# A unit's second scan and its B placed ahead of the sums' eviction, and the last pair's output reordered, in a fused Mamba-2 and SiLU kernel

## The chip, the cores and the metric

The kernel runs on one core of a Trainium2 chip. The metric is the device time of one execution in microseconds. The kernel before takes 362.78 us, the median of three runs (362.65, 362.78 and 364.97). The execution that the profile shows took 364.51 us as a whole; its span in the profile is 362.7 us.

## The reference

Two blocks follow each other. The first is a chunked state-space scan with decays `a` over 768 positions for 4 batches and 8 heads (head size 32, state size 16). The second is a feed-forward block with a SiLU over the 3072 tokens, with 256 features and 2048 hidden ones.

```
cum = cumsum(log a);  L[i, j] = exp(cum[i] - cum[j]) for i >= j
M = (C B^T) * L
y = M x + (C state) * exp(cum)                     # within a chunk, and from the state
state = exp(cum[-1]) * state + sum_j exp(cum[-1] - cum[j]) B[j] x[j]
...
h = y @ w_in;  g = h * sigmoid(h);  out = g @ w_out    # per token, y with all heads side by side
```

The activations and the output are 32-bit floats; the weights come as 64-bit floats and are read as pairs of 32-bit words, from which ACT, DVE and GpSimd make 32-bit floats.

## The kernel before, in words

The tokens are cut into 12 **units** of 256 positions, three to a batch; two units are a **pair** of 512 tokens. The scan of a unit makes the feed-forward block's input `XF`. The first pair (P = 0) has a path of its own. For pairs 1 to 5 a loop `step(s)` runs over s = 0 to 82: s = 16 (P - 1) + f handles the 128 hidden features number f of pair P, and in the gaps it is interleaved with the scan of the two units of the next pair, called "a" and "b". The order of the instructions on each engine is the order in which this Python code emits them; nothing reorders it. The table `PLAN` names by f what is emitted for the scan, `FIRST` does so for "2B" alone.

**The products.** Each matrix product with exact 32-bit operands is split in three single-pass ones. A value v is split into a high part h, a low part l = v - h, and a third operand d, a sum of the two with other weights. With h h', l l' and d d' the wanted product comes out as a weighted sum. In `step`:

- `s1_h` (L526) and `s1_d` (L518) are the first matrix product, on TensorE; `hp` is its PSUM tile, which ACT rescales between the two (L520).
- `s1_g` (L534, L536) is SiLU and the high part of its result on ACT; `s1_gl` (L540) and `s1_gd` (L544) make the low part and the d part. In some steps (`ASIDE`: f = 2, 4, 5, 6, 10, 15) `s1_gl` is on GpSimd, else on DVE.
- `s2` (L558, L559) adds h h' and l l' of the second product into the two PSUM tiles `OA[P][m]`, three steps later (`LAG`). `s2_d` (L572) adds d d' of it into the tile `B2[P]`, which covers four PSUM banks. While scans need these banks, the d d' products of some steps are put off and collect in `PENDING`.

`B2` and the scan's tiles `gy` share these four banks, one tile at a time.

**The end of a pair.** When the sixteenth `s2` of a pair is due, `ends` is true: that is at f = 2 of the next pair, s = 18, 34, 50, 66 and, for the last pair, 82. `f_out` then evicts the sums on DVE. For pairs 1 to 4 the part of `B2` up to then was set aside at f = 8 by ACT as `SUM2` (`f_sum2`, L580), so that the bank could be used by the scan; L595 computes UP * OA - SUM2, and L602 subtracts what `B2` gathered since. For the last pair no `SUM2` exists, so ACT copies OA with its scale (L598) in place of L595, and L602 follows. `f_store` transposes the two results on DVE (L611) and stores each with four DMAs on the SP queue (L613). It comes at f = 5 for the pairs before the last, and at once for the last. For the first pair `f_out0` at s = 2 does it, with a copy on ACT (L584), transposes and stores.

**The scan of a unit.** `f_E1` is half of the E scan (a running product per head, L324, on DVE, 128 x 512 from the tile `ab`). For unit "a" the first half is emitted at f = 1 and the second at f = 3 ("2B" in `FIRST`); for "b" the first at f = 8 and the second at f = 9. Behind the second half comes `f_B` (L347), which makes BT from B and the last columns of E. BT is the weight of the state products `f_D0` (L390), which `PLAN` has at f = 3 (a) and f = 9 (b), behind `f_G` (L402). Then follow the state steps on DVE (L422), the product with E on DVE (`f_M`, L408), and the output products of `f_Y` (L442, L451) at f = 5 and 11. The loads of the next unit are emitted with their waits on the SP queue ("bL" at f = 1): `bn` waits until BT has been read, `ab` until the scan has been done.

Within `step`, the order before is: `s1_h`, `s1_d`; at an end the outstanding d d' products, `s2` and `f_out`; `s1_g`; else `s2` and, where due, `s2_d`; `f_sum2`; the `FIRST` part; `s1_gl`, `s1_gd`; the stores; the `PLAN` parts; splitting of weights.

Of the kernel before, what the change touches and what calls it, by code (L numbers as in the profile page):

```python
# [12 lines left out]
AF = mybir.ActivationFunctionType  # L13
ALU = mybir.AluOpType
# [14 lines left out]
UP = 4097.0  # L29
# [4 lines left out]
def kernel(  # L34
# [22 lines left out]
    nc = tc.nc  # L57
# [27 lines left out]
    def block(name, dtype=FP32):  # L85

        return blk.tile([128, 512], dtype, name=name, tag="blk", bufs=NB)

    def half(name):
        return ps_h.tile([128, 512], FP32, name=name, tag="h")  # L90

    def bank4(name="gy"):
        return ps_s.tile([128, 4, 512], FP32, name=name, tag="gy")

    def acc(name):
        return ps_a.tile([128, 512], FP32, name=name, tag="a")

    ab, bn, tbc, xt = ({} for _ in range(4))
# [40 lines left out]
    def load_unit(u):  # L139
        load_pa(u, nc.sync)  # L140
        if 0 < u < UPB:
            load_n(u, 1, nc.sync)
        else:
            load_t(u, 0, nc.sync)
            load_t(u, 1, nc.sync)
        load_n(u, 0, nc.sync)
        load_ab(u, nc.sync)
        load_x(u, nc.sync)
# [10 lines left out]
    def two(t):  # L159
        return t.rearrange("p (k f) -> p k f", k=2)  # L160
# [195 lines left out]
    def f_TP(u):  # L356
        tp = half("tp")
        for i, t in enumerate((bn[u],) if u == 0 else (bn[u], tbc.pop(u))):
            for k in range(2):
                nc.tensor.transpose(out=tp[:, 256 * i + 128 * k:256 * i + 128 * k + 128],  # L360
                                    in_=t[:, k].rearrange("p h n -> p (h n)"), identity=ident)
        BH[u] = sc.tile([128, UT], FP32, name="bh")
        nc.scalar.activation(BH[u], tp[:, 0:256], AF.Copy)
        if u > 0:
            CT[u] = tp[:, 256:512]

    def f_T2(u, e):
        if e == 0:
            CE[u] = sc.tile([128, 2, UT], FP32, name="ce")
        nc.scalar.activation(CE[u][:, e], CT[u], AF.Copy, scale=par[:, e:e + 1])  # L370
# [114 lines left out]
    GT, OA = {}, {}  # L485
# [28 lines left out]
    def s1_d(s):  # L514
        P, f = 1 + s // NF, s % NF
        HP[s] = half("hp")
        for kc in range(KC):
            nc.tensor.matmul(out=HP[s], lhsT=two(WD[f // 2])[:, kc, 128 * (f % 2):128 * (f % 2) + 128], rhs=XD[P][:, kc],  # L518
                             start=(kc == 0), stop=False, skip_group_check=True)
        nc.scalar.activation(HP[s], HP[s], AF.Copy, scale=-HALF / UP)  # L520
# [26 lines left out]
    B2, SUM2 = {}, {}  # L547

    def s2(s):

        P, f = 1 + s // NF, s % NF
        if f == 0:
            OA[P] = [acc("oa") for m in range(2)]
        n, r = 8 + f // 2, f % 2
        gh, gl = GH.pop(s), GL.pop(s)
        for m in range(2):
            ms = slice(128 * m, 128 * m + 128)
            nc.tensor.matmul(out=OA[P][m], lhsT=two(WH[n])[:, r, ms], rhs=gh, start=(f == 0), stop=False)  # L558
            nc.tensor.matmul(out=OA[P][m], lhsT=two(WL[n])[:, r, ms], rhs=gl, start=False, stop=(f == NF - 1))  # L559

    def s2_d(tiles):

        P = 1 + tiles[0] // NF
        fresh = P not in B2
        if fresh:
            B2[P] = bank4("b2")
        for s in tiles:
            f = s % NF
            n, r = 8 + f // 2, f % 2
            gd = GD.pop(s)  # L570
            for m in range(2):
                nc.tensor.matmul(out=B2[P][:, m], lhsT=two(WD[n])[:, r, 128 * m:128 * m + 128], rhs=gd,  # L572
                                 start=(fresh and s == tiles[0]), stop=True, skip_group_check=True)

    def f_sum2(P):

        b2 = B2.pop(P)
        SUM2[P] = [block("sum2") for m in range(2)]
        for m in range(2):
            nc.scalar.activation(SUM2[P][m], b2[:, m], AF.Copy, scale=HALF)  # L580
# [8 lines left out]
    def f_out(P):  # L589

        b2 = B2.pop(P)
        for m in range(2):
            o = block("o")
            if P in SUM2:
                nc.vector.scalar_tensor_tensor(out=o, in0=OA[P][m], scalar=UP, in1=SUM2[P][m],  # L595
                                               op0=ALU.mult, op1=ALU.subtract)
            else:
                nc.scalar.activation(o, OA[P][m], AF.Copy, scale=UP)  # L598
            OUT.append((P, m, o))
        for m in range(2):  # L600
            o = OUT[m][2]
            nc.vector.scalar_tensor_tensor(out=o, in0=b2[:, m], scalar=-HALF, in1=o, op0=ALU.mult, op1=ALU.add)  # L602

    def f_store():
        for P, m, o in OUT:
            store(P, m, o)
        OUT.clear()

    def store(P, m, o):
        r = block("ot")  # L610
        nc.vector.transpose(out=r, in_=o)  # L611
        for q in range(4):
            nc.sync.dma_start(  # L613
                out=bass.AP(tensor=out.tensor, offset=out.offset + 2 * UT * P * d_model + 128 * m + 32 * q,
                            ap=[[d_model, 32], [32 * d_model, 2 * UT // 32], [1, 32]]),
                in_=r[32 * q:32 * q + 32].rearrange("p (b d) -> p b d", d=32))
# [60 lines left out]
    def stage(u, what):  # L677
        for c in what:
            if c == "L":
                load_unit(u)  # L680
            elif c == "T":
                if 0 < u < UPB:
                    f_TP(u)
                else:
                    f_T(u, 0)
                    f_T(u, 1)
                f_T2(u, 0)
                f_T2(u, 1)
            elif c == "P":
                f_P(u)  # L690
            elif c in "12":
                f_E1(u, int(c) - 1, 2)
            elif c == "B":
                f_B(u)
            elif c == "C":
                f_C(u)
            elif c == "D":
                f_G(u)
                f_D0(u)
            elif c == "M":  # L700
                f_M(u, 0)
                f_M(u, 1)
            elif c == "S":
                f_S(u)
            elif c == "s":
                f_SM(u)
            elif c == "Y":
                f_Y(u)
                f_X(u)
            elif c == "h":  # L710
                f_xh(u)
            elif c == "l":
                f_xl(u)
            elif c == "d":
                f_xd(u)
# [17 lines left out]
    for text in ("m0 3:C12B 2:h h1 l0 d0 2:l b13 s14", "m1 3:D 2:d 4:L h2 l1 d1 b14 s15", "m2 3:SsM h3 l2 d2 b15",  # L733
# [4 lines left out]
    NP = NU // 2  # L738
# [1 line left out]

    PLAN = {0: ("aPC",), 1: ("a1", "bL"), 3: ("aD",), 4: ("aSsM",), 5: ("aY",), 6: ("ah", "bT"), 7: ("bPC",), 8: ("b1", "aL"),
            9: ("bD",), 10: ("bSsM",), 11: ("bY",), 12: ("bh", "ald"), 13: ("bld",), 15: ("aT",)}
    FIRST = {3: "a2B", 9: "b2B"}

    ASIDE = (2, 4, 5, 6, 10, 15)
    PENDING = []
# [3 lines left out]
    def step(s):  # L750

        last = NF * (NP - 1)
        t = s - LAG
        P, f = 1 + s // NF, s % NF
        ends = t >= 0 and t % NF == NF - 1
        scans = P + 1 < NP
        if t >= 0:
            PENDING.append(t)
        if s == 0:
            s1_d(0)  # L760

        if s < last:
            s1_h(s)
            if s + 1 < last:
                s1_d(s + 1)
        if ends:
            s2_d(PENDING)
            s2(t)
            PENDING.clear()
            f_out(1 + t // NF)  # L770
        if s < last:
            s1_g(s)
        if s < 2:
            f_s2(6 + s)
        if s == 2:
            f_out0(0)
            f_out0(1)
        if t >= 0 and not ends:
            s2(t)
        if PENDING and not (scans and (f < 6 or 9 <= f < 12)):  # L780
            s2_d(PENDING)
            PENDING.clear()
        if scans and f == 8:
            f_sum2(P)
        if scans and f in FIRST:
            stage(2 * P + 2 + "ab".index(FIRST[f][0]), FIRST[f][1:])
        if 1 <= s <= last:
            s1_gl(s - 1, nc.gpsimd if f in ASIDE and scans else nc.vector)
            s1_gd(s - 1)
        if ends and s >= last:  # L790
            f_store()
        if s >= last:
            return
        if t > 4 and t % NF == 2:
            f_store()
        if scans:
            for what in PLAN.get(f, ()):
                u = 2 * P + 2 + "ab".index(what[0])
                if f == 15 or what == "aL":
                    u += 2  # L800
                if u < NU:
                    stage(u, what[1:])
        if s in PARTS:
            w_h(PARTS[s])
        if s - 1 in PARTS:
            w_l(PARTS[s - 1])
            w_d(PARTS[s - 1])
# [34 lines left out]
```

## Time and profile before

| engine | busy us | share of 362.7 us |
|---|---|---|
| PE (matmul) | 333.4 | 92% |
| PEld (weight load) | 260.3 | 72% |
| DVE | 259.7 | 72% |
| ACT | 211.7 | 58% |
| POOL (GpSimd) | 64.4 | 18% |

A group's row in the profile gives line, engine, operation, what is written and read, count, busy time, mean ns, idle time of the engine ahead of these instructions and what ended it. These are the groups that the change touches:

```profile
L324 DVE TENSOR_TENSOR_SCAN E<-ab,diag 128x512 f32<-128x512 f32 x24 | 29.2, 1232 | 1.1 <-DMA ab<-a_zero 0.6 <-PE ab L331 0.5
L347 DVE TENSOR_TENSOR BT<-bn,E 128x256 f32<-128x256 f32 x12 | 8.8, 732 | 0.4
L595 DVE SCALAR_TENSOR_TENSOR o<-oa,sum 128x512 f32<-128x512 f32 x8 | 5.2, 686 | 10.3 <-PE oa L559 10.3
L580 ACT ACTIVATE sum<-b 128x512 f32<-128x512 f32 x8 | 4.3, 585 | 0.0
```

A busy PE isn't a PE at its peak, since matmuls are pipelined: a 128 x 512 product is recorded with some 0.39 us, while the next one starts 0.23 us later. The end of the span holds no matmuls: the last one starts at 353.29 us.

### The profile page before, as it was taken

How to read it: one execution, taken by the hardware profiler on the slowest of the kernel's cores; microseconds unless marked ns; L12 is line 12 of the kernel's file. 1: busy time of each engine (PE TensorE's matmuls, PEld its weight loads, DVE VectorE, ACT ScalarE, POOL GpSimd, SP SyncE). 2: the span in 40 equal slices, each digit the busy share in tenths (PEclk: the TensorE clock that was granted, in tenths of full speed). 3: DMA queues.
4: the chain of work that ended last, by engine and by line, in shares of the span. 5: the costliest groups of instructions: out<-in, count | busy, mean ns of one | idle time of the engine just before them, and what ended most of it. 6: DMA issues, size and time to landing. Idle time of an engine off the chain costs nothing.

```text
span 362.7 us, 7826 instructions
## 1 busy us (share of the span) xinstructions
PE 333.4 (92%) x3145; PEld 260.3 (72%) x3146; DVE 259.7 (72%) x430; ACT 211.7 (58%) x403; POOL 64.4 (18%) x56
## 2 busy tenths in 40 slices
PE   8888999897979999979999979999979999999990
PEld 3567787776747778757778757777758778788870
DVE  6969976995388998697865685865684863574442
ACT  3566576144348876747666637667636766656630
POOL 3225441220113011122101132101131101000000
PEclk9999999898989999999999989999989999999997
DMA  6875976521026240135330143420153000030003
GB/s 140 181 260 147 223 263 135 125 65 27 16 46 118 55 94 0 37 64 108 76 73 0 43 100 67 96 49 2 43 109 54 2 2 0 0 52 7 0 3 59
DMA packets 99339, 26.67 MB, mean 74 GB/s; under 512 B 87558, under 2 KB 92422, under 8 KB 99302
## 3 DMA queue, kind: packets, MB, share of 16 engines
q1 hardware_dynamic: 97222, 26.03, 31.7%
q8 instruction: 25, 0.41, 0.5%
q10 hardware_dynamic: 2080, 0.13, 0.4%
q14 instruction: 12, 0.10, 0.1%
HBM read 22.80 MB, written 3.34 MB: 72 GB/s over the span
## 4 chain that ended last, share of the span: by engine, by line
PE 67%; DVE 14%; SPq 6%; DMA 6%; issue 3%; ACT 1%; DVEq 0%; ACTq 0%
PE hp L526 21%; PE b L572 10%; PE hp L518 10%; PE oa L559 10%; PE oa L558 10%; DMA raw<-in_moe_w_out_dram 3%; DVE E L324 2%; PE oa L504 2%; SPq L121 2%; DVE wv L187 2%; PE gy L451 2%; DVE BT L347 2%; PE gy L442 1%; DVE wl L203 1%; DMA raw<-in_moe_w_in_dram 1%
## 5 line engine op out<-in xcount | busy, mean ns | idle before, releaser
L520 ACT ACTIVATE hp<-hp 128x512 f32<-128x512 f32 x80 | 46.6, 582 | 90.2 <-PE hp L518 89.9
L540 DVE TENSOR_TENSOR gl<-g,gh 128x512 fp32r<-128x512 f32 x56 | 38.6, 690 | 52.3 <-ACT gh L536 47.2
L540 POOL TENSOR_TENSOR gl<-g,gh 128x512 fp32r<-128x512 f32 x24 | 38.1, 1589 | 188.4 <-ACT gh L536 183.6
L526 PE MATMUL hp<-xh,wh 128*128 128x512 f32 x160 | 66.6, 416 | 2.6 <-ACT hp L520 2.6
L544 DVE SCALAR_TENSOR_TENSOR gd<-gh,g 128x512 fp32r<-128x512 f32 x80 | 57.8, 726 | 9.8 <-ACT gh L536 9.7
L526 PE MATMUL hp<-xl,wl 128*128 128x512 f32 x160 | 64.5, 403 | 0.0
L559 PE MATMUL oa<-gl,wl 128*128 128x512 f32 x160 | 64.4, 402 | 0.0
L558 PE MATMUL oa<-gh,wh 128*128 128x512 f32 x160 | 63.8, 399 | 0.0
L536 ACT ACTIVATE gh<-g 128x512 fp32r<-128x512 f32 x80 | 50.5, 632 | 2.9
L518 PE MATMUL hp<-xd,wd 128*128 128x512 f32 x160 | 52.1, 407 | 0.0
L534 ACT ACTIVATE g<-hp 128x512 f32<-128x512 f32 x80 | 47.5, 594 | 0.6 <-PE hp L526 0.6
L572 PE MATMUL b<-gd,wd 128*128 128x512 f32 x160 | 44.6, 391 | 0.0
L526 PEld LDWEIGHTS hp<-xh,wh 128*128 128x128 f32 x160 | 30.7, 192 | 12.8 <-ACT hp L520 5.4
L518 PEld LDWEIGHTS hp<-xd,wd 128*128 128x128 f32 x160 | 31.0, 194 | 7.7
L558 PEld LDWEIGHTS oa<-gh,wh 128*128 128x128 f32 x160 | 30.9, 193 | 7.8 <-ACT o L584 0.7
L559 PEld LDWEIGHTS oa<-gl,wl 128*128 128x128 f32 x160 | 30.8, 193 | 7.5
L572 PEld LDWEIGHTS b<-gd,wd 128*128 128x128 f32 x160 | 30.0, 188 | 6.8 <-DVE o L602 0.2
L526 PEld LDWEIGHTS hp<-xl,wl 128*128 128x128 f32 x160 | 30.7, 192 | 5.8
L491 PE MATMUL hp<-xf,w 128*128 128x256 f32 x128 | 30.2, 386 | 3.6 <-POOL w L192 2.1
L192 POOL TENSOR_TENSOR w<-wu,wv 128x512 uint32<-128x512 uint32 (+1 forms) x20 | 23.4, 1179 | 50.5 <-DVE wv L187 47.8
L504 PE MATMUL oa<-gT,w 128*128 128x256 f32 x128 | 31.0, 402 | 0.0
L491 PEld LDWEIGHTS hp<-xf,w 128*128 128x128 f32 x128 | 23.4, 190 | 9.2 <-POOL w L192 3.4
(80 smaller groups left out, 370.3 us busy)
## 6 DMA issues: line engine op xcount, KB each, us to landing
ab<-a_zero SPq DMA_DIRECT2D x40, 128.0 KB
raw<-in_moe_w_in_dram SPq DMA_DIRECT2D x8, 512.0 KB
raw<-in_moe_w_out_dram SPq DMA_DIRECT2D x8, 512.0 KB
xt<-in_x_dram SPq DMA_DIRECT2D x24, 128.0 KB
out_dram<-ot SPq DMA_DIRECT2D x48, 64.0 KB
bn<-in_B_dram SPq DMA_DIRECT2D x22, 64.0 KB
tbc<-in_C_dram SPq DMA_DIRECT2D x40, 32.0 KB
pz<-a_in SPq DMA_DIRECT2D x40, 32.0 KB
```

Of the source, the lines that this page charges most:

```text
L491: nc.tensor.matmul(out=hp[:, i], lhsT=two(w32[j])[:, kc, 128 * i:128 * i + 128], rhs=two(XF[u])[:, kc], start=(kc == 0), stop=(kc == KC - 1))
L504: nc.tensor.matmul(out=OA[0][m][:, UT * u:UT * u + UT], lhsT=two(w32[8 + j])[:, i, 128 * m:128 * m + 128], rhs=two(GT[u, j])[:, i], start= ...
L518: nc.tensor.matmul(out=HP[s], lhsT=two(WD[f // 2])[:, kc, 128 * (f % 2):128 * (f % 2) + 128], rhs=XD[P][:, kc], start=(kc == 0), stop=Fals ...
L520: nc.scalar.activation(HP[s], HP[s], AF.Copy, scale=-HALF / UP)
L526: nc.tensor.matmul(out=HP[s], lhsT=two(w[f // 2])[:, kc, 128 * (f % 2):128 * (f % 2) + 128], rhs=x_[P][:, kc], start=False, stop=(kc == KC ...
L534: nc.scalar.activation(G[s], HP.pop(s), AF.Silu, scale=UP)
L536: nc.scalar.activation(GH[s], G[s], AF.Copy, scale=DOWN)
L540: engine.tensor_tensor(out=GL[s], in0=G[s], in1=GH[s].bitcast(FP32), op=ALU.subtract)
L544: nc.vector.scalar_tensor_tensor(out=GD[s], in0=GH[s].bitcast(FP32), scalar=1.0 + 1.0 / HALF, in1=G.pop(s), op0=ALU.mult, op1=ALU.subtract)
L558: nc.tensor.matmul(out=OA[P][m], lhsT=two(WH[n])[:, r, ms], rhs=gh, start=(f == 0), stop=False)
L559: nc.tensor.matmul(out=OA[P][m], lhsT=two(WL[n])[:, r, ms], rhs=gl, start=False, stop=(f == NF - 1))
L572: nc.tensor.matmul(out=B2[P][:, m], lhsT=two(WD[n])[:, r, 128 * m:128 * m + 128], rhs=gd, start=(fresh and s == tiles[0]), stop=True, skip ...
```

## The change

The first part moves the `FIRST` block of a step ahead of the block for the end of a pair, and moves "a2B" from f = 3 to f = 2. So the second half of a unit's E scan and its BT are emitted one step earlier and stand on DVE ahead of the eviction of the sums (and, at s = 2, ahead of the first pair's transposes). "b2B" stays at f = 9 and only moves within the step. What this is for: BT is to be there when `f_D0` needs it at f = 3.

The second part is the last pair's output. At s = 81 both outstanding steps' d d' products are emitted behind that step's `s2`, and `f_sum2` sets their sum aside on ACT. At s = 82 the last `s2` follows, and `f_end` does, for each half m in turn, one subtraction (as in L595), the transpose, and four stores on two queues, SP and ACT. This replaces the copy on ACT (L598), the L602 of this pair and the stores on SP alone. `f_out` loses its branch for the last pair.

```diff
@@ f_out
-            if P in SUM2:
-                nc.vector.scalar_tensor_tensor(out=o, in0=OA[P][m], scalar=UP, in1=SUM2[P][m],
-                                               op0=ALU.mult, op1=ALU.subtract)
-            else:
-                nc.scalar.activation(o, OA[P][m], AF.Copy, scale=UP)
+            nc.vector.scalar_tensor_tensor(out=o, in0=OA[P][m], scalar=UP, in1=SUM2[P][m],
+                                           op0=ALU.mult, op1=ALU.subtract)
             OUT.append((P, m, o))
...
+    def f_end(P):
+
+        for m in range(2):
+            o = block("o")
+            nc.vector.scalar_tensor_tensor(out=o, in0=OA[P][m], scalar=UP, in1=SUM2[P][m],
+                                           op0=ALU.mult, op1=ALU.subtract)
+            store(P, m, o, (nc.sync, nc.scalar))
...
-    def store(P, m, o):
+    def store(P, m, o, queues=(nc.sync,)):
         r = block("ot")
         nc.vector.transpose(out=r, in_=o)
         for q in range(4):
-            nc.sync.dma_start(
+            queues[q % len(queues)].dma_start(
...
-    FIRST = {3: "a2B", 9: "b2B"}
+    FIRST = {2: "a2B", 9: "b2B"}
@@ step, behind s1_h and s1_d
+        if scans and f in FIRST:
+            stage(2 * P + 2 + "ab".index(FIRST[f][0]), FIRST[f][1:])
+        if s == last + 1:
+            s2(t)
+            s2_d([t, t + 1])
+            f_sum2(NP - 1)
+            return
+        if s == last + 2:
+            s2(t)
+            f_end(NP - 1)
+            return
         if ends:
             s2_d(PENDING)
             s2(t)
...
-        if scans and f in FIRST:
-            stage(2 * P + 2 + "ab".index(FIRST[f][0]), FIRST[f][1:])
         if 1 <= s <= last:
             s1_gl(s - 1, nc.gpsimd if f in ASIDE and scans else nc.vector)
             s1_gd(s - 1)
-        if ends and s >= last:
-            f_store()
         if s >= last:
             return
```

## The prediction

> **What bounds the kernel now.** I read the page first, then the waits, then the timeline around the longest waits, then one answer of windows, and last the timeline of the end. The page says that TensorE is the bound: it is busy for 92% of the span, and it holds 67% of the chain that ended last. DVE holds another 14%, and that is what one can win.
>
> ```profile
> PE 333.4 (92%) x3145; PEld 260.3 (72%) x3146; DVE 259.7 (72%) x430; ACT 211.7 (58%) x403; POOL 64.4 (18%) x56
> PE 67%; DVE 14%; SPq 6%; DMA 6%; issue 3%; ACT 1%; DVEq 0%; ACTq 0%
> ```
>
> The waits (engine and line, what it waited for: us in total, times, longest) name the one place in the steady loop where TensorE waits long: the state products of L390 wait for BT of L347. From 100 to 350 us it is the only row of PE itself, 9.3 us in 4 times. In the same step DVE waits in front of the eviction (L595) for TensorE, 10.3 us, of which three waits of 2.29 and one of 3.41 us, and once 7.1 us in front of the first pair's transposes.
>
> ```profile
> PE gy L390 <- DVE BT L347: 11.2, 5, 2.5
> DVE o L595 <- PE oa L559: 10.3, 4, 3.4
> DVE ot L611 <- ACT o L584: 7.1, 1, 7.1
> ```
>
> So two engines wait for each other in turn. The timeline (start, us, engine, line, operation, count, idle before) shows one of the four places, first DVE, then PE:
>
> ```profile
> 149.83 1.22 DVE L324 TENSOR_TENSOR_SCAN E<-ab,diag 128x512 f32<-128x512 f32 x1
> 153.33 1.29 DVE L595 SCALAR_TENSOR_TENSOR o<-oa,sum 128x512 f32<-128x512 f32 x2 [2.29 <-PE oa L559]
> 154.54 1.28 DVE L602 SCALAR_TENSOR_TENSOR o<-b,o 128x512 f32<-128x512 f32 x2
> 155.73 0.68 DVE L544 SCALAR_TENSOR_TENSOR gd<-gh,g 128x512 fp32r<-128x512 f32 x1
> 156.33 1.22 DVE L324 TENSOR_TENSOR_SCAN E<-ab,diag 128x512 f32<-128x512 f32 x1
> 157.59 1.30 DVE L347 TENSOR_TENSOR BT<-bn,E 128x256 f32<-128x256 f32 x1
> ...
> 156.00 0.69 PE L402 MATMUL gy<-ce,bh 32*64 32x128 f32 x32
> 158.94 0.46 PE L390 MATMUL gy<-xt,BT 64*32 64x64 f32 x32 [2.24 <-DVE BT L347]
> ```
>
> DVE is idle from 151.05 to 153.33. Then it does the eviction, a gd, the scan and BT in one run, and TensorE stands still from 156.69 to 158.94. The scan's own input needs neither the sums nor TensorE. The windows (us, busy of PE, PEld, DVE, ACT and POOL, granted clock, DMA share, GB/s) show what follows three of the four gaps:
>
> ```profile
> 102.42:104.96 2.54, 0.01 (x1) 0.00 (x0) 2.51 (x4) 0.75 (x2) 1.29 (x1) 1.00 0.00 0
> 105.90:109.32 3.42, 3.42 (x10) 2.64 (x9) 3.31 (x9) 1.51 (x3) 0.00 (x0) 0.52 0.73 147
> 156.69:158.94 2.25, 0.01 (x1) 0.00 (x1) 2.22 (x3) 0.24 (x1) 1.54 (x1) 1.00 0.04 7
> 158.94:162.35 3.41, 3.41 (x45) 2.69 (x46) 3.30 (x9) 1.29 (x3) 0.00 (x0) 1.00 0.57 91
> 209.02:211.27 2.25, 0.00 (x2) 0.00 (x1) 2.22 (x3) 0.24 (x1) 1.60 (x1) 1.00 0.03 7
> 211.72:215.14 3.42, 3.42 (x9) 2.64 (x10) 3.25 (x8) 0.71 (x2) 0.00 (x0) 0.52 0.60 114
> ```
>
> After the gaps at 102.42 and 209.02 (and after the one at 262.86, 2.25 us, not shown) the clock is 0.52 for 3.4 us; after that at 156.69 it stays 1.00. The slow stretches begin at 105.90, 211.72 and 266.34. Their distances, 105.82 and 54.62, are 31 and 16 times 3.414, so they lie on a grid. A grid line near 157.10 cuts the second gap into 0.41 and 1.84 us; the other three lie in one period each.
>
> The end, after the last matmul:
>
> ```profile
> 353.32 1.08 ACT L598 ACTIVATE o<-oa 128x512 f32<-128x512 f32 x2 [3.81 <-PE oa L559]
> 353.96 1.29 DVE L602 SCALAR_TENSOR_TENSOR o<-b,o 128x512 f32<-128x512 f32 x2 [3.11 <-ACT o L598]
> 355.16 1.29 DVE L611 STREAM_TRANSPOSE ot<-o 128x512 f32<-128x512 f32 x2
> 355.89 4.10 SPq L613 DMA_DIRECT2D out_dram<-ot  x8
> ```
>
> Eight stores follow each other on one queue for 4.10 us, 0.51 each, and the span ends 2.7 us after the last one.
>
> **What the Trainium skill says.** "TensorE: Matmul & The Clock Gate", Part 1, "What's actually happening": the array's clock is halved after an idle window of a free-running 3413 ns period. The trace agrees on the half (0.52) and the period (3.414 from the distances); it differs on the amount, since here 2.25 us of idle inside one period were enough, and 1.84 were not. "SBUF — State Buffer", "SBUF: two separate sides": a DVE operation with two SBUF inputs and a GpSimd operation exclude each other for the whole instruction. The trace agrees: BT is 0.43 us at its shortest and 1.30 at 157.59, where a GpSimd gl runs from 157.06 to 158.60. "DMA: Bandwidth & Descriptors", "Issuing engines are not separate DMA queues": a second issuing engine saves only the issue time. In the trace issue is just what limits the end: while the eight stores run, the DMA engines' share is 0.66 to 0.76.
>
> **The change, part by part.**
>
> (1) Scan and BT at f = 2 instead of f = 3. At steps 18, 34 and 50, DVE now has the scan and BT ahead of L595, in its 2.29 us of idle. Alone they are 1.22 + 0.43 = 1.65 and end at 152.70. The GpSimd gl of the step starts at 150.99 and takes 1.29, so one of the two may be held up until it ends at 152.28; then BT ends near 153.65 and the eviction starts up to 0.35 late. Queued behind it are L595 and L602; the next step's L558 (154.99) waits for L595, which had 0.7 us to spare; f_G (L402) waits for L602, which in the trace costs 0.36 already. So the gap of 2.25 closes and 0 to 0.35 comes back at f_G; I take 0.15: 2.1 each, 6.3 in three places. At step 2 there is no eviction of this kind; DVE is idle from 93.42 to 100.56 ahead of the transposes, so all 2.54 us go. Sum **8.8** (bounds 8.2 to 9.3).
>
> (2) The clock. If no gap of more than 0.7 us is left, the three slow stretches go too. Each costs 3.42 x (1 - 0.52) = 1.6 us, as TensorE was busy through it. The profiled execution took 364.51 us, the median is 362.78: 1.73 lower, about one stretch less. So I count two for the median: **3.2** (bounds 0 to 4.8).
>
> (3) At f = 9 nothing stands on DVE between the old and the new place, nor on TensorE; 0, as the order on every engine is the same. Loads of the next unit, which wait for BT and the scan, start some 5 us earlier; they were not waited for.
>
> (4) The end. TensorE's order is unchanged: two d' products come before the last four sums as before, and gd of the last step is done at 350.84, ahead of their start at 351.71. New on ACT: two SUM2 copies at 0.585 (row of L580) from about 352.6, beside the last four matmuls. Gone: the two copies of L598 and two of the four DVE passes over PSUM. DVE can start at 353.35 in place of 353.96 and does o, ot, o, ot: about 2.6, so the first ot ends near 354.65, the second near 355.95 (before: 355.86 and 356.45). Stores: four from 354.7 and four from 356.0, two on each queue, 0.5 each: the last issue ends at 357.05 in place of 359.99, **2.9** earlier. The data bound it from the other side: 0.52 MB at 131 GB/s / 0.76 = 172 GB/s for all engines busy takes 3.05 us; from 355.5 (the first data came some 0.8 after the issue) that ends at 358.6 against 361.0: 2.4. I take **2.6**.
>
> Sum 8.8 + 3.2 + 2.6 = 14.6, and 362.8 - 14.6 = **348.2 us**.
>
> **The rivals.** (a) Slack of DVE runs out, or the clock still dips. In the first pair DVE is busy for 47.65 of 54.33 us (105 to 159.33). With the gap and the dip gone TensorE does this in about 50.4, and the products of L451 wait for the E product of L408, which had 1.5 us to spare at 111.7 and would have none. If the 3.2 of the clock do not come: 351.4. (b) The GpSimd lock costs more, and f_G's wait for L602 takes the place of the wait for BT: half of the gaps, one dip and the end, 4.4 + 1.6 + 2.6: 354.2. Against it stands that DVE's work in the step is the same, so it cannot be late by more than 0.35. (c) Only the end gains, as the gaps come back elsewhere: 360.2. (d) Slower: the moved scan has to wait for its ab load and holds back the eviction and with it the sums of the next step. A delay of 2 us in four places, less the end, and two more slow stretches: 362.8 + 8 - 2.6 + 3.2 = 371.4. The waits speak against it: scans waited for a load once, 0.6 us, in another part of the kernel, and the first half of the same load was already read one step earlier.
>
> **How the numbers follow.** Forecast 0.60, (a) 0.20, (b) 0.12, (c) 0.05, (d) 0.03. With the best bounds of each term (9.3 + 4.8 + 2.9) it is 345.8; the clock stretches of the start (two before 90 us) can add or take one, so I go to 345.0. Upward the range holds (a) and most of what lies between it and (b): 353.5. Faster by over 1% (below 359.2) are the forecast, (a) and (b): 0.92; same is (c): 0.05; slower 0.03.
>
> **What would show it.** In the profile after: the row of L390 waiting for BT gone from PE's waits; the scan and BT ahead of L595; BT between 0.43 and 1.3; f_G's wait for L602 at most 0.7; no clock of 0.5 between 100 and 345 us; two rows of stores, on SP and on ACT, of about 2 us each. The prediction is wrong if PE waits for L602, L595 or L408 by more than 1 us in a place, or if slow stretches turn up without gaps.

## The result, and the profile after

The changed kernel takes **349.51 us**, the median of four runs (348.75 to 349.82), beside 362.73 us for the kernel before (now the median of four runs): a ratio of 0.9618, with a 95% interval from 0.9578 to 0.9658. The forecast was 348.2 us, its range 345.0 to 353.5.

First the same two parts of the page as before, of the changed kernel: engines, and the chain that ended last.

```profile
PE 324.6 (94%) x3145; PEld 254.3 (73%) x3146; DVE 262.6 (76%) x430; ACT 211.9 (61%) x403; POOL 66.1 (19%) x56
PE 70%; DVE 10%; DMA 8%; SPq 8%; issue 2%; ACT 1%; DVEq 0%; ACTq 0%
```

PE works through the same 3145 matmuls in 8.8 us less busy time, so part of the gain is speed, not idle time. The page's row of the clock, of the kernel before and then of the changed one, says where the speed comes from:

```profile
PEclk9999999898989999999999989999989999999997
PEclk9999999999999999999999999999999999999998
```

Before, five slices stand at 8. Two of them lie ahead of 100 us, where the change does nothing: such stretches come and go from one execution to the next. The other three follow gaps in the loop. Now no slice is below 9 but the last, whose matmuls end 1.6 us into it. From the waits of the changed kernel between 100 and 340 us (waiting line, releaser: us, times, longest):

```profile
PE gy L442 <- DVE E L408: 1.4, 1, 1.4
DVE o L594 <- PE oa L559: 3.4, 1, 3.4
DVE ot L616 <- ACT o L584: 5.0, 1, 5.0
```

The first line is all that PE itself waits for in this time: the row of L390 waiting for BT is gone there. DVE's three waits of 2.29 us in front of the eviction (L594 now) are gone as well, and only the one of step 66 is left, where no scan is due. But there is a new wait, at L442. Step 18 in the timeline, DVE and then PE:

```profile
145.50 2.33 DVE L324 TENSOR_TENSOR_SCAN E<-ab,diag 128x512 f32<-128x512 f32 x2
147.87 1.34 DVE L347 TENSOR_TENSOR BT<-bn,E 128x256 f32<-128x256 f32 x1
149.13 1.27 DVE L594 SCALAR_TENSOR_TENSOR o<-oa,sum 128x512 f32<-128x512 f32 x2
150.33 1.27 DVE L599 SCALAR_TENSOR_TENSOR o<-b,o 128x512 f32<-128x512 f32 x2
...
151.69 0.69 PE L402 MATMUL gy<-ce,bh 32*64 32x128 f32 x32
152.31 0.46 PE L390 MATMUL gy<-xt,BT 64*32 64x64 f32 x32
```

Both scan halves run back to back, BT is ready at 149.2, and L390 follows L402 without a wait. The step began at 145.57, so the eviction comes 3.56 us into the step; it was 3.44. The end, and below it the DMA windows (us; busy of PE, PEld, DVE, ACT, POOL; clock; DMA share, GB/s):

```profile
338.63 1.08 ACT L580 ACTIVATE sum<-b 128x512 f32<-128x512 f32 x2 [3.35 <-PE b L572]
339.27 0.69 DVE L605 SCALAR_TENSOR_TENSOR o<-oa,sum 128x512 f32<-128x512 f32 x1 [2.65 <-ACT sum L580]
339.99 0.71 DVE L616 STREAM_TRANSPOSE ot<-o 128x512 f32<-128x512 f32 x1
340.63 0.65 DVE L605 SCALAR_TENSOR_TENSOR o<-oa,sum 128x512 f32<-128x512 f32 x1
340.73 2.20 SPq L618 DMA_DIRECT2D out_dram<-ot  x4
340.74 2.31 ACTq L618 DMA_DIRECT2D out_dram<-ot  x4
...
342.00:343.00 1.00, 0.00 (x0) 0.00 (x0) 0.03 (x1) 0.00 (x0) 0.00 (x0) 1.00 1.17 188
343.00:344.00 1.00, 0.00 (x0) 0.00 (x0) 0.00 (x0) 0.00 (x0) 0.00 (x0) 0.53 1.26 201
```

From the end of the last matmul (353.68 before, 339.44 now) to the end of the span it is 9.05 us before and 7.04 now.

**Where the time went, stage by stage.** The start of the kernel scatters: over the twelve profiles of this study the first f_G of the loop (L402 at s = 3) starts between 99.6 and 102.6 us, in code that is nearly the same in all of them. So stages say more than totals here. From that f_G to the end of the last matmul it is 251.95 us before and 239.30 after, and 239.30 in a second profile of the changed kernel. The 12.6 us between them all lie in four places, from the start of f_G at f = 3 to the start of f_Y at f = 5:

| f_G to f_Y, us | pair 1 | pair 2 | pair 3 | pair 4 | sum |
|---|---|---|---|---|---|
| before | 10.01 | 8.18 | 9.68 | 9.72 | 37.6 |
| before, gap filled (below) | 8.68 | 8.18 | 8.16 | 8.18 | 33.2 |
| after | 7.30 | 5.86 | 5.85 | 5.91 | 24.9 |

### The profile page after: what moved, and what is told of

It reads as the page before. It is cut to its first block, busy times and chain, and to the rows that moved or that the text cites. A ratio compares the mean times of both kernels' runs of the same rounds, so it can differ in the third digit from the quotient of the medians.

```text
span 346.5 us, 7826 instructions
## 1 busy us (share of the span) xinstructions
PE 324.6 (94%) x3145; PEld 254.3 (73%) x3146; DVE 262.6 (76%) x430; ACT 211.9 (61%) x403; POOL 66.1 (19%) x56
## 4 chain that ended last, share of the span: by engine, by line
PE 70%; DVE 10%; DMA 8%; SPq 8%; issue 2%; ACT 1%; DVEq 0%; ACTq 0%
PE hp L526 22%; PE b L572 11%; PE hp L518 10%; PE oa L559 10%; PE oa L558 10%; DMA raw<-in_moe_w_out_dram 3%; SPq L121 3%; PE oa L504 2%; DVE wl L203 2%; PE gy L451 2%; DMA ab<-a_zero 2%; PE gy L442 1%; DMA a_in<-acl 1%; DMA raw<-in_moe_w_in_dram 1%; PE gy L402 1%
## 5 line engine op out<-in xcount | busy, mean ns | idle before, releaser
L540 POOL TENSOR_TENSOR gl<-g,gh 128x512 fp32r<-128x512 f32 x24 | 39.9, 1663 | 172.4 <-ACT gh L536 156.3
L526 PE MATMUL hp<-xh,wh 128*128 128x512 f32 x160 | 65.6, 410 | 2.6 <-ACT hp L520 2.6
L544 DVE SCALAR_TENSOR_TENSOR gd<-gh,g 128x512 fp32r<-128x512 f32 x80 | 61.9, 776 | 6.0 <-ACT gh L536 6.0
L526 PE MATMUL hp<-xl,wl 128*128 128x512 f32 x160 | 63.2, 395 | 0.0
L559 PE MATMUL oa<-gl,wl 128*128 128x512 f32 x160 | 63.1, 394 | 0.0
L558 PE MATMUL oa<-gh,wh 128*128 128x512 f32 x160 | 62.7, 392 | 0.0
L518 PE MATMUL hp<-xd,wd 128*128 128x512 f32 x160 | 50.4, 396 | 0.0
L558 PEld LDWEIGHTS oa<-gh,wh 128*128 128x128 f32 x160 | 30.0, 188 | 7.5 <-ACT o L584 0.7
L518 PEld LDWEIGHTS hp<-xd,wd 128*128 128x128 f32 x160 | 30.0, 188 | 7.3
L324 DVE TENSOR_TENSOR_SCAN E<-ab,diag 128x512 f32<-128x512 f32 x24 | 28.7, 1228 | 0.7 <-DMA ab<-a_zero 0.7
```

Of the source, the lines that this page charges most:

```text
L324: nc.vector.tensor_tensor_scan(out=E[u].rearrange("p k h t -> p (k h t)")[:, Q * g0:Q * (g0 + n)], data0=t.rearrange("p g t -> p (g t)"), ...
L526: nc.tensor.matmul(out=HP[s], lhsT=two(w[f // 2])[:, kc, 128 * (f % 2):128 * (f % 2) + 128], rhs=x_[P][:, kc], start=False, stop=(kc == KC ...
L540: engine.tensor_tensor(out=GL[s], in0=G[s], in1=GH[s].bitcast(FP32), op=ALU.subtract)
L544: nc.vector.scalar_tensor_tensor(out=GD[s], in0=GH[s].bitcast(FP32), scalar=1.0 + 1.0 / HALF, in1=G.pop(s), op0=ALU.mult, op1=ALU.subtract)
```

## The experiments

| run | median us (n) | before on that chip | ratio, 95% interval |
|---|---|---|---|
| scan part alone | 350.83 (4) | 363.78 | 0.9666, 0.9618 to 0.9714 |
| end part alone | 360.31 (8) | 363.78 | 0.9926, 0.9892 to 0.996 |
| scan at f = 2, behind the eviction | 359.23 (10) | 363.78 | 0.9882, 0.9847 to 0.9917 |
| before, gap filled | 359.08 (4) | 363.78 | 0.9891, 0.9843 to 0.9939 |
| after, split later | 348.83 (6) | 363.67 | 0.9598, 0.9556 to 0.9639 |
| the same, gl of f = 4 on DVE | 348.07 (6) | 363.67 | 0.9581, 0.9538 to 0.9623 |
| after again | 351.02 (6) | 363.67 | 0.9646, 0.961 to 0.9683 |
| after, one queue | 349.69 (6) | 363.67 | 0.9613, 0.9578 to 0.9648 |
| first hp earlier | 348.91 (6) | 363.49 | 0.959, 0.9552 to 0.9628 |
| the same, one queue | 348.35 (6) | 363.49 | 0.9587, 0.9545 to 0.963 |

**Each part of the change alone.** The scan part:

```diff
-    FIRST = {3: "a2B", 9: "b2B"}
+    FIRST = {2: "a2B", 9: "b2B"}
...
+        if scans and f in FIRST:
+            stage(2 * P + 2 + "ab".index(FIRST[f][0]), FIRST[f][1:])
         if ends:
...
-        if scans and f in FIRST:
-            stage(2 * P + 2 + "ab".index(FIRST[f][0]), FIRST[f][1:])
```

> The kernel before with the first part of the change alone (second half of a unit's scan and its BT ahead of the end of a pair, at f = 2); the end is as before. Theory (the scan's place closes four gaps of PE and takes the half clock behind them away; the end is a separate gain of 2.0 us, read from the two traces): 362.7 - 13.2 + 2.0 = 351.5 us, and no wait of L390 for BT in the loop. Rival (the end brings more than its trace shows, or the two parts need each other): 354 or more.

The end part, whose `f_end` stores on SP and ACT:

```diff
+        if s == last + 1:
+            s2(t)
+            s2_d([t, t + 1])
+            f_sum2(NP - 1)
+            return
+        if s == last + 2:
+            s2(t)
+            f_end(NP - 1)
+            return
         if ends:
```

> The kernel before with the second part alone (d d' of both last steps together, their sum set aside on ACT, one pass per half, stores on SP and ACT). Theory: 362.7 - 2.0 = 360.7 us, the four waits of L390 for BT as before. Rival: 358.5 or less if the end is worth what part (4) of the prediction gave as its upper bound and more; 362.7 if the output stores were hidden anyway.

Both came within 0.7 us of their number. But the kernel before ran 1 us slower on that chip than the 362.7 us that the numbers start from: beside it the parts gained 13.0 and 3.5 us, where 11.2 and 2.0 were expected. Both expected gains lie within the intervals, so the medians don't show that the parts add up. The stages do: the scan part alone has 239.29 us from f_G to the last matmul and 8.68 behind it; the end part alone has 252.00 and 6.74. The stage behind the last matmul varies too, by 0.4 us: three kernels with the old end have 9.05, 9.04 and 9.05 us. So the parts don't need each other, and the scan part is nearly the whole gain. Its profile still has the wait of 1.4 us at L442, so that wait belongs to the scan part.

**Is it the step, or the place within the step?** The same `FIRST`, with the block left where it was, so that scan and BT stand behind the eviction on DVE:

```diff
-    FIRST = {3: "a2B", 9: "b2B"}
+    FIRST = {2: "a2B", 9: "b2B"}
```

> The kernel before with a2B at f = 2 but in its old place within the step, so that on DVE it stands behind the eviction (L595, L602) and behind the first pair's transposes. Theory (what counts is that the scan fills DVE's idle time ahead of the eviction): the scan ends some 0.65 us earlier than before where a pair ends, as only one gd no longer stands ahead of it, so gaps of 0.8 to 1.6 us are left in all four places; 2.6 to 5.6 us of gap saved, and with gaps below 1.84 us the slow clock goes too (3.2): 354 to 357 us. Rival (the step alone counts, the order within it does not): 351.5 us as with the first part of the change.

It took 359.23 us: far from the rival's 351.5, so the place within the step does count, but slower than the theory's 354 to 357. Its ten runs differ: three took 356.9 to 357.4 us at a mean granted clock of 0.989 or 0.990, the other seven 358.9 to 361.2 at 0.977 to 0.984. The profile is of one of the seven. In pairs 2 to 4 the theory holds: f_G to f_Y is 7.32, 7.08 and 7.37 us, 1.2 to 1.5 us more than in the changed kernel and without a slow stretch. The first pair went wrong. In PE's timeline and then in the windows of this run:

```profile
110.23 1.13 PE L442 MATMUL gy<-cw,sm 32*64 32x64 f32 x32 [2.92 <-DVE E L408]
...
107.30:110.20 2.90, 0.01 (x1) 0.00 (x0) 2.79 (x8) 1.59 (x4) 0.00 (x0) 0.95 1.13 168
109.90:113.30 3.40, 3.07 (x98) 2.71 (x99) 3.40 (x5) 2.33 (x6) 1.46 (x1) 0.50 0.56 97
113.30:116.70 3.40, 3.40 (x9) 2.63 (x9) 2.41 (x5) 1.69 (x4) 0.00 (x0) 0.50 0.01 1
```

PE reaches f_Y while DVE still works off its queue, waits 2.92 us there, and the clock is halved for two periods of 3.41 us from 109.91 on. It is the wait of the changed kernel, twice as long.

**Is the slow clock caused by the gap?** In the kernel before, the gap is filled with products whose result nothing reads:

```diff
+    FILL = [0]
+
     def stage(u, what):
...
                 f_G(u)
+                if FILL[0]:
+                    for i in range(FILL[0]):
+                        nc.tensor.matmul(out=DP[u][:, i % 4, 384:512], lhsT=ident, rhs=ident, start=True, stop=True,
+                                         skip_group_check=True)
                 f_D0(u)
...
         if scans:
+            FILL[0] = 9 if f == 3 else 0
             for what in PLAN.get(f, ()):
```

> The kernel before with nine products of the 128 x 128 identity with itself (4-byte operands) between f_G (L402) and f_D0 (L390) at f = 3, into columns of the PSUM tile that nothing reads; they take about 0.21 us each, 1.9 us, and lie in the gap in which PE waits for BT, so the gap stays and PE is busy in it. Theory (the half clock comes from PE's idle time): the gaps stay, no slow stretch between 100 and 345 us, 362.7 - 3.2 = 359.5 us. Rival (the slow stretches come on their own grid whatever PE does, or from the load): slow stretches as before and 362.7 us.

The windows of this run show the filled stretch in pair 3 and then the time behind it, and that behind the filler in pairs 1 and 4:

```profile
208.00:213.00 5.00, 4.96 (x82) 4.19 (x72) 4.93 (x8) 0.90 (x3) 1.60 (x1) 1.00 0.23 22
213.00:216.40 3.40, 3.40 (x41) 2.46 (x44) 3.30 (x6) 3.34 (x8) 1.77 (x1) 1.00 0.70 182
...
106.00:109.40 3.40, 3.40 (x46) 2.64 (x27) 3.33 (x8) 1.49 (x3) 0.00 (x0) 1.00 0.59 105
...
267.00:270.40 3.40, 3.40 (x105) 2.62 (x104) 3.40 (x5) 2.78 (x7) 2.37 (x2) 1.00 0.77 156
```

The clock is 1.00 throughout, and there is no slow stretch between 100 and 345 us. All four runs have a mean granted clock of 0.984 to 0.991, the 17 of the kernel before beside them 0.971 to 0.980. The run takes 359.08 us, near the theory's 359.5, though PE waits at least as long for useful work; beside the kernel before on that chip it gains 4.7 us, more than the 3.2 that the theory counted. So idle time is the cause, and the table above splits the gain: 37.6 - 33.2 = **4.4 us** for three slow stretches (1.33, 1.52 and 1.54), and 33.2 - 24.9 = **8.3 us** for the gaps.

Which gaps draw a stretch changes from run to run: in the profile of the end part alone it is those in pairs 1, 2 and 4. The clock records of the twelve profiles show what decides it. In each profile the slow stretches begin on a grid of periods of 3.413 us, and the grid lies differently in each execution. The gap in pair 3 of the end part alone, 2.25 us, is cut by a grid line into 0.69 and 1.56. Added up for each period from 10 us on, PE's recorded idle time nearly separates the two cases: all 17 periods with 1.88 us or more were followed by a slow one. Of the others, with 1.86 us or less, one was: it has 1.69 us and begins at 72.36 in the run with the scan behind the eviction. The same run's second slow period in a row follows one with only 0.33 us of idle time; why is open.

**What the new wait is.** In the changed kernel DVE's queue ahead of the product with E in the first pair is this:

```profile
101.97 1.78 DVE L203 SCALAR_TENSOR_TENSOR wl<-wh,w 128x512 fp32r<-128x512 f32 x1
103.67 0.68 DVE L208 SCALAR_TENSOR_TENSOR wd<-wh,w 128x512 fp32r<-128x512 f32 x1
104.27 0.68 DVE L544 SCALAR_TENSOR_TENSOR gd<-gh,g 128x512 fp32r<-128x512 f32 x1
104.87 1.22 DVE L422 SCALAR_TENSOR_TENSOR st<-st,pfx,gy 128x64 f32<-128x64 f32 x4
106.01 1.28 DVE L408 TENSOR_TENSOR E<-gy,E 128x512 f32<-128x512 f32 x2
```

The pass of 1.78 us takes 0.68 elsewhere; it overlaps a gl that GpSimd runs from 101.74 on. Two edits try to take this away, the first by moving the weight's split, the second by moving the gl of f = 4 too (`ASIDE` belongs to the second alone):

```diff
-    PARTS = {0: 9, 2: 10, 4: 11, 5: 6, 6: 12, 8: 7, 9: 13, 11: 14, 13: 15}
+    PARTS = {0: 9, 3: 10, 4: 11, 5: 6, 6: 12, 8: 7, 9: 13, 11: 14, 13: 15}
...
-    ASIDE = (2, 4, 5, 6, 10, 15)
+    ASIDE = (2, 5, 6, 10, 15)
```

> The changed kernel with the splitting of one weight tile (w_h, w_l, w_d of tile 10) one step later, so that in the first pair its two DVE passes (1.78 and 0.68 us, the first held up by a GpSimd gl) stand behind the products with E (L408) and not ahead of them. Theory (the first pair has no slack left on DVE: f_Y waits there 1.35 us for L408, plus 0.36 of PE's weight loads, and this wait is what is missing from the forecast): the wait goes, 1.3 to 1.7 us faster than the changed kernel, 348 us. Rival (DVE is late by the amount of its whole work there, so that the wait only moves to the next product, or it is not on the path): within 0.4 us of the changed kernel.

> As e6_split_later, and the gl of f = 4 on DVE instead of GpSimd in every pair. Theory (a GpSimd gl that meets DVE work with two SBUF inputs holds it up by some 1.1 us, more than the 0.69 us which gl takes on DVE): 0 to 0.5 us faster than e6_split_later, and no pass of 1.78 us ahead of the products with E at f = 4. Rival (DVE is the tighter engine there and the lock costs nothing on the path): slower than e6_split_later by up to 0.7 us in each pair.

> The changed kernel as it is, beside the others on the same chip: 349.5 us, the measure for e6_split_later, e10_split_gl and e7_one_queue.

By the medians, both would be gains, 2.2 and 3.0 us over the run beside them. The stages, in one profile of each, say that most of it is the start's scatter. From f_G to the last matmul it is 239.14 and 238.86 us, against 239.30: **0.2 and 0.4 us**. Of the waits in PE's timeline, first those of the kernel with the split later, with unit b's product with E on DVE below them:

```profile
106.28 0.69 PE L442 MATMUL gy<-cw,sm 32*64 32x64 f32 x32 [0.16 <-DVE E L408]
126.80 0.69 PE L442 MATMUL gy<-cw,sm 32*64 32x64 f32 x32 [0.94 <-ACT hp L520]
125.37 1.28 DVE L408 TENSOR_TENSOR E<-gy,E 128x512 f32<-128x512 f32 x2
```

and then that of the changed kernel beside it:

```profile
108.67 0.69 PE L442 MATMUL gy<-cw,sm 32*64 32x64 f32 x32 [1.38 <-DVE E L408]
126.56 1.28 DVE L408 TENSOR_TENSOR E<-gy,E 128x512 f32<-128x512 f32 x2
```

The first f_Y comes 6.09 us after f_G in place of 7.31, as intended, but the next f_Y, of unit b, at 26.61 in place of 26.80: it waits 0.94 us where it didn't wait before. The profile names ACT as the last releaser there, but unit b's L408 ends only 0.02 us ahead of that pass, and it ends 26.5 us after f_G in both kernels: DVE gets there no earlier. So the rival of that run was right: the wait only moved. Between 101.15 and 151.70 us of the changed kernel's first profile DVE is busy for 47.60 of 50.55 us; in the first pair it carries the splitting of the weights besides all else. With the gl of f = 4 on DVE, no pass of 1.78 us is left ahead of L408, and the stage is 0.3 us shorter again; that supports the lock as a cost of this size, no more.

**The second queue.** The changed kernel with all eight stores on SP:

```diff
-            store(P, m, o, (nc.sync, nc.scalar))
+            store(P, m, o)
```

> The changed kernel with the last pair's eight stores on the SP queue alone. Theory (with two queues the DMA engines bound the end, with one the issue of 0.5 us each does): the last issue ends at about 340.7 + 8 x 0.51 = 344.8 instead of 343.05, the data come at the 131 GB/s of before, and the run is 1.4 us slower than the changed kernel. Rival (the earlier first store is the whole gain, the second queue none): the same as the changed kernel.

The median, 349.69 us, is not above the 351.02 of the changed kernel on the same chip, and the intervals overlap. The trace of this run shows why one would expect a difference. Stores, and DMA in the windows:

```profile
340.44 4.10 SPq L618 DMA_DIRECT2D out_dram<-ot  x8
...
341.00:342.00 1.00, 0.00 (x0) 0.00 (x0) 0.71 (x1) 0.00 (x0) 0.00 (x0) 1.00 0.52 90
342.00:343.00 1.00, 0.00 (x0) 0.00 (x0) 0.00 (x0) 0.00 (x0) 0.00 (x0) 1.00 0.67 115
343.00:344.00 1.00, 0.00 (x0) 0.00 (x0) 0.00 (x0) 0.00 (x0) 0.00 (x0) 0.72 0.72 124
```

The data take 4.27 us in place of 2.86 to 2.91, and the last lands 6.40 us after the last matmul in place of 5.0. But from the last data to the end of the span it is 1.47 us in this profile and 2.0 us in both of the changed kernel; why is not shown. From the last matmul to the end of the span: 7.88 against 7.04. So of the 2.0 us that the end part gains in the profile, 1.2 come without the second queue.

To see it in the times, I tried to make the start scatter less, in the kernel with the split later and the gl of f = 4 on DVE:

```diff
-                 "m3 3:Y h4 l3 d3", "m4 3:h h5 l4 d4 h8 3:l", "m5 3:d l5 d5 4:T l8 d8"):
+                 "m3 3:Y h4 l3 d3", "m4 3:h h5 l4 d4 h8 3:l", "m5 3:d l5 d5"):
         todo(text)
...
         if s == 0:
             s1_d(0)
+            todo("4:T l8 d8")
```

> As e10_split_gl, and on ACT the first rescaling of hp (L520 of s = 0) ahead of the two ce copies (L370) which wait for DVE; nothing else moves. Theory (a gap of PE costs itself and, when it fills most of one clock period, 1.6 us more): the gap of 1.94 us at 83.3 us, in which PE waits for this L520, shrinks by about 1.2 us and no slow stretch follows it: 1.2 to 2.8 us faster than e10_split_gl, 346 us, and a smaller spread of the runs. Rival (PE waits for the next thing at once): the same as e10_split_gl.

> As e11_first_hp with the last pair's eight stores on SP alone, to measure the second queue with a smaller spread than e7_one_queue had. Theory (from the traces of the changed kernel and of e7_one_queue: last data 1.4 us later, end of the span 0.85 us later): 0.85 us slower than e11_first_hp. Rival (the second queue is worth nothing in the time, as the times of e7_one_queue have it): the same or faster.

This failed as an aid and as a gain. The gap in front of the first `s1_h` is 0.67 us in both profiles with the edit; but it is 0.67 in four of the ten profiles without it too, and 1.94 to 1.97 in the other six, so that the edit shrinks it was not shown. The run is no faster than without it (348.91 against 348.07 us, on two chips; 0.9590 against 0.9581 of the kernel before on each), and its six runs still spread over 3 us: its profile has two slow stretches before 70 us, in a part that the edit doesn't touch. One queue again came out no slower (348.35), while its trace has 7.84 us behind the last matmul in place of 7.21. The second queue shortens the profiled end by 0.6 to 0.85 us; that it shortens the execution was not shown.

No version beats the changed kernel beyond the intervals. The best is the one with the split later and the gl of f = 4 on DVE, and of its 3.0 us only 0.4 lie in the stages that it changes.

## Why the prediction was right

The range held the time, and the mechanism was the one forecast: the gaps closed, and the slow clock behind them went. The sum by parts, 14.6 us, stands beside 12.64 + 2.01 = 14.7 us in the two profiles' stages, but that it comes so close is luck: the terms were off by -0.5, +1.2 and -0.6 us, which cancel. The medians differ by 13.2 us; the rest is within the scatter of the start.

- **Scan and BT ahead of the eviction: 8.8, measured 8.3.** In pairs 2 to 4 the gap of 2.25 us went whole, 2.3 us each: f_G's wait for the eviction stayed at 0.36 us. The 0.15 us per place that I set aside for the GpSimd lock were hardly paid. The exclusion of DVE and GpSimd that the Trainium skill states ("SBUF — State Buffer", "SBUF: two separate sides") was there: GpSimd's gl took 2.26 us at 146.67, beside the second scan, and BT 1.34 behind it. But GpSimd had the slack, and the eviction came only 0.12 us later in its step. The error is in the first pair: the step "all 2.54 us go" held at f_G, but 1.35 us came back two steps later at f_Y. Rival (a) had named it: "would have none".
- **The clock: 3.2, measured 4.4.** The mechanism was right, as the filled gap shows. The size was off by one stretch: counted as three, the prediction's own 1.6 us each would have given 4.8. I took the profiled execution, 1.73 us above the median, to have one stretch more than the median. The profiles of this study have three in the loop both times that the gaps were left open (the kernel before, and the end part alone), and the scatter lies in the start. Each cost 1.33 to 1.54 us rather than 1.6. The prediction's windows stood 0.12 us ahead of the clock records, so that 0.52 is 0.50 in these. The grid line near 157.10 is at 157.22 and cuts the second gap into 0.53 and 1.72 us; lines cut two of the other gaps as well, and leave 2.35 and 2.07 us in one period. On the idle time that it takes, the runs stand against the Trainium skill, "TensorE: Matmul & The Clock Gate", Part 1, "What's actually happening", which names a whole idle window of about 3.4 us: here 1.88 us within one period were enough.
- **The end: 2.6, measured 2.0.** The two copies of SUM2 started only when all four products of d d' were done (338.63), so that the first pass over OA waited for ACT: it started 0.18 us ahead of the last matmul's end, not 0.33. The bound from the data was right to 0.15 us (2.91 us for 3.05). What I left out is that the end of the span could move behind the last data: it was 2.0 us in place of 1.7. The rule of the Trainium skill, "DMA: Bandwidth & Descriptors", "Issuing engines are not separate DMA queues", that a second issuing engine saves only issue time, holds: the second queue saved it, which showed in the data because issue had been the limit (the data took 2.9 us in place of 4.27), and 0.6 to 0.85 us of it reached the end.
- **b2B at f = 9: 0.** Its place on DVE is as before, and no wait of L390 shows there.

Of the marks named in the prediction, the row of L390, the order on DVE, f_G's wait, the clock and the two rows of stores all came as written; BT took up to 1.34 us where 1.3 was named. The one that was to speak against it, a wait of PE for L408 of more than 1 us, came too, once.

## What to carry to other kernels

When two engines wait for each other in turn within one step, look for work of the late one that needs nothing of the other and put it into its idle time ahead of the exchange; the same move to behind the exchange brought 4.6 us here in place of 13.0. Price a gap of TensorE with what the clock does after it: three gaps of 2.2 to 2.5 us cost 4.4 us more than their own length, and filling them with products that nothing reads got that part back. When the start of a kernel scatters by more than the effect, compare the stages of the profiles, since two of the edits here looked like 2 and 3 us in the median and were 0.2 and 0.4 in the stages.

## What I had not expected

- From f_G at s = 3 to the last matmul, the four profiles with the scan part and no other change to the loop agree to 0.1 us (239.29, 239.30, 239.30 and 239.37), while the time ahead of it moves by 1.6 us among them and by 2.9 us over all twelve profiles.
- TensorE needn't be idle for a whole period to lose half its clock for the next one: 1.88 us of 3.41 were enough, and a gap of 2.25 us escaped where a grid line cut it in two.
- A wait that had been closed at one f_Y opened at the next (1.38 to 0.16 us at the first, 0 to 0.94 at the second): with DVE busy for 94% of a stage, a new order moved the wait but didn't take it away.
- With stores on two queues the end of the span comes 2.0 to 2.2 us after the last data in five profiles and 1.75 in the sixth (the end part alone), with one queue 1.4 to 1.7 in six.
